# A planned one-core transformer block: other engine costs in the planner, and x tiles 4 and 5 transposed by DMA

## The chip, the cores and the metric

The kernel runs on one core of one Trainium2 chip. A core has five engines with a queue each: PE (TensorE, matmuls), ACT (ScalarE), DVE (VectorE), POOL (GpSimd) and SP (SyncE, which here only issues DMAs). An engine takes its instructions strictly in the order in which they were written into its queue; a wait at the head of a queue holds up all that stands behind it. The metric is the device time of one execution in microseconds.

## The reference

One block over 2048 tokens of width 1024, in bf16: multi-query attention with 32 heads of width 32 and one shared K and V, then a gated feed-forward part of width 3584.

```
h  = x + softmax(q k^T * 32**-0.5) v @ wo        # q, k, v from layernorm(x); k and v have one head
h2 = h + (sigmoid(g) * u) @ w_down               # g, u from layernorm(h) @ w_gate, w_up
```

## The kernel before

**Tiles.** There are 16 token tiles of 128. The first layer norm (`stats`, L325, with `ph` 0) takes tiles of x, and each normalised tile is transposed, either by PE over a PSUM bank (`mk_xT`) or by a DMA transpose (`x_by_dma`, L378, which first scales the tile on DVE). `TUNE["xd"]` says from which tile on the DMA does it: 6 before. From the transposed tiles come K and V (`mk_KV`) and Q (`mk_Qc` for the first two tiles, `mk_Q` for the others, which go out to `q_scratch` and are read back).

**Attention.** One "visit" is one key tile for half of the heads of one token tile. PE computes four score matmuls of 512 columns, which run side by side on four groups of 32 rows of the array (`emit_S`), into two of three pairs of PSUM banks; ACT does two exps of 1024 columns (L662), which write P to one of 12 slots of `Pr` (a few other buffers serve as slots at first); DVE adds the slot to `acc` (L637). There are 2 x 16 visits a token tile and 512 in all. Every eight key tiles, P·V (`mk_PV`) runs four matmuls side by side on four groups of 32 columns, and its result is taken into `oun` (L753, L757). At the end of each half the sums go through PE (`mk_SUM`), a reciprocal on DVE (L699), a write to `r_scratch` and four broadcast reads into `rb` (L702), and `OT` is the product (L716). The first two halves take their sums from matmuls with ones instead.

**The rest of a token tile.** The out-projection `mk_OP` adds to x in `h_sb` (L819). The second layer norm is `stats` with `ph` 1: bn_stats and bn_aggr, two casts (`mvb` L340, `mvr` L342) on DVE; eps, square root and reciprocal on POOL (`zb` L344, `dsb` L347, `rstd` L350); `hn` on DVE (L825); a DMA transpose to `hnT` (L840). The gate and up matmuls (`mk_GU`, here "gate/up") take seven groups of weights a tile from a ring of slabs in SBUF, which are loaded anew for nearly each tile (L902); ACT does tanh (L955) and DVE the product `hact` (L961). The down matmuls (`mk_D`, "down") are four groups of 28 a tile, added to `h_sb` (L998), and go out by L1005.

**Who sets the order.** None of this order is written by hand. `Plan` runs once while the program is built: it keeps for each engine the time from which it is free, gives every operation an occupancy and a latency in ns, and puts it into its engine's list. The four other engines always take the ready operation that can start first, by priority. PE's list is made by the loop at the end: a visit goes in as soon as the exp that frees its banks is known to have ended and ACT has less than `run` (900 ns) of work ahead; in between, PE is filled from the queues of groups (`PRIOS`, `held`), matmul by matmul, and each change of mode between plain, row-tiled and column-tiled matmuls adds `SWITCH`. Two PSUM banks, `F_ps`, serve all groups but the scores. So a wrong cost in the planner leaves no error in the result, only an order that meets waits the planner did not see. Numbers that matter here:

- the occupancy and latency of the three POOL steps, L343 to L352;
- `SWITCH` (L150), and `LATE` (L45), which adds ns to the landing of some DMAs by their key: `rb`, `hT`, `xt` (the keys of the slabs begin with `sl`, that of `r_scratch` is `rd`, but keys are compared without trailing digits);
- `h0`, `h1`: while a long group is about to end, DVE work of low priority (the adds) is held if it would overlap the stretch from `h0` to `h1` ns after that end;
- `qf`: which order of queues PE is filled from; `few`, `sum_few`, `pv_few`: at how many free P slots P·V and sums may interrupt or start outside the row mode; `swait`: how long PE may stay in column mode for a visit; `d_a`, `d_b`: when the down groups are due; `dall`: whether a down group waits for all of its weights; `eb`, `eq`: a bias in ns on the choice between ACT and DVE for emptying PSUM in the head.

Of the kernel before, what the change touches and what calls it, by code (L numbers as in the profile page):

```python
# [15 lines left out]
SEM = 75.0  # L16


TUNE = dict(swait=200, parts=2, raw=2, rl=0, nd=4, pc=16, rate=270, pace=280, xd=6, qf=0, dall=1, wo_late=1,
            nkn=3, few=2, rmin=700, hmin=1, h0=100, h1=100, hf=1.0, run=900, sum_few=2, pv_few=3, d_off=2,  # L20
            d_a=0, d_b=1, eb=450, eq=1000)


class Op:
# [16 lines left out]
class Plan:  # L41


    ENG = ("act", "dve", "pool", "sp")
    LATE = {"rb": 300.0, "hT": 400.0, "xt": 400.0}  # L45

    def __init__(self):
        self.lists = {e: [] for e in ("pe",) + self.ENG}
# [44 lines left out]
    def step(self, limit):  # L93
# [21 lines left out]
        if o.nbytes:  # L115
            if o.pace:
                self.pace_free = s + o.nbytes / TUNE["pace"]
            go = max(s + 1500.0, self.dma_free)
            self.dma_free = go + o.nbytes / TUNE["rate"]
            o.end = self.dma_free + 750.0 + self.LATE.get(o.key.rstrip("0123456789"), 0.0)  # L120
        else:
# [25 lines left out]
    return dict(occ=n / rate + fix - 90.0, lat=n / rate + fix + SEM)  # L147


SWITCH = 97.0  # L150


def bass_sequential_preLN__grouped_kv_mqa__glu_gated_glu__prompt_kernel(
# [16 lines left out]
    NT = S // P  # L170
# [13 lines left out]
    with ExitStack() as es:  # L184
# [3 lines left out]
        def SB(name, shape, dt=BF16):  # L188
            return EC(nc.sbuf_tensor(name, [P] + shape, dt))
# [13 lines left out]
        rb = SB("rb", [512], F32)  # L203
# [52 lines left out]
        def evac(fn_act, fn_dve, n, deps, prio, dve_rate=0.96, bias=0.0):  # L256
            now = pl.free["pe"]
            a = max(pl.free["act"], now) + sum(o.occ for o in pl.heap["act"]) + n / 1.2 + bias
            d = max(pl.free["dve"], now) + sum(o.occ for o in pl.heap["dve"] if o.prio <= prio) + n / dve_rate
            if a < d:  # L260
                return pl.op("act", fn_act, deps, prio=min(prio, 2), **t_act(n))
            return pl.op("dve", fn_dve, deps, prio=prio, **t_dve(n, dve_rate))

        def both(out_ap, in_ap):
            return (lambda: ACT.activation(out=out_ap, in_=in_ap, func=ACTF.Copy),
                    lambda: DVE.tensor_copy(out=out_ap, in_=in_ap))  # L266
# [57 lines left out]

        def stats(ph, tiles, srcs, deps, prio):  # L325
            t0, k = tiles[0], len(tiles)
            ag = []
            for t, src, dp in zip(tiles, srcs, deps):
                s = n_st[0] % 8
                n_st[0] += 1  # L330
                a = pl.op("dve", lambda s=s, src=src: DVE.bn_stats(st[:, s, 0, :], src[:, 0:512]), dp, prio=prio,  # L331
                          occ=600, lat=756, order=[st_user.get(s)])
                b = pl.op("dve", lambda s=s, src=src: DVE.bn_stats(st[:, s, 1, :], src[:, 512:1024]), dp, prio=prio,  # L333
                          occ=600, lat=756, order=[st_user.get(s)])
                c = pl.op("dve", lambda s=s, t=t: DVE.bn_aggr(mv[:, ph, t, :], st[:, s, :, :]), [a, b], prio=prio - 1,
                          occ=110, lat=284)
                st_user[s] = c
                ag.append(c)
            tk = slice(t0, t0 + k)
            d = pl.op("dve", lambda: DVE.tensor_copy(out=mvb[:, ph, tk, :], in_=mv[:, ph, tk, :]), ag, prio=prio - 1,  # L340
                      occ=90, lat=250)
            e = pl.op("dve", lambda: DVE.tensor_copy(out=mvr[:, ph, tk, :], in_=mvb[:, ph, tk, :]), [d], prio=prio - 1,  # L342
                      occ=90, lat=250)  # L343
            f = pl.op("pool", lambda: POOL.tensor_scalar(  # L344
                out=zb[:, ph, tk], in0=mvb[:, ph, tk, 1], scalar1=LN_EPS_BF16, scalar2=None, op0=ALU.add),
                [d], prio=prio - 1, occ=330, lat=440)
            g = pl.op("pool", lambda: POOL.tensor_tensor(  # L347
                out=dsb[:, ph, tk], in0=zb[:, ph, tk], in1=half[:, 0:k], op=ALU.pow), [f, c0], prio=prio - 1,
                occ=460 + 180 * k, lat=560 + 180 * k)
            h = pl.op("pool", lambda: POOL.tensor_tensor(  # L350
                out=rstd[:, ph, tk], in0=dsb[:, ph, tk], in1=negone[:, 0:k], op=ALU.pow), [g, c1], prio=prio - 1,
                occ=400 + 180 * k, lat=500 + 180 * k)  # L352
            return e, h

        sv1 = {}
        for tiles in ([0], [1], [2, 3], [4, 5], [6, 7], [8, 9], [10, 11], [12, 13], [14, 15]):
            r = stats(0, tiles, [x_sb(t) for t in tiles], [[x_ld[t]] for t in tiles], 3)
            for t in tiles:
                sv1[t] = r
        xnorm = {}  # L360
        xcent = {}
        for t in range(NT):
            if t >= TUNE["pc"]:
                xcent[t] = pl.op("pool", lambda t=t: POOL.tensor_scalar(
# [7 lines left out]
        def make_norm1(t, deps):  # L372
            dst, src, sc = xn[:, t % 2, :], x_sb(t), rstd[:, 0, t:t + 1]
            xnorm[t] = evac(lambda: ACT.activation(out=dst, in_=src, func=ACTF.Copy, scale=sc),
                            lambda: DVE.tensor_scalar(out=dst, in0=src, scalar1=sc, scalar2=None, op0=ALU.mult),
                            1024, [xcent[t], sv1[t][1]] + deps, 1, 3.2, bias=TUNE["eb"])

# [34 lines left out]
        def pe_op(fn, n, mode, deps, last_of_round=True):  # L412
            if mode != pl.pe_mode:
                pl.free["pe"] += SWITCH
                pl.pe_mode = mode
# [10 lines left out]
        def mk_xT(t):  # L426
# [6 lines left out]
            def after(b, last):  # L433
                src = F_ps[:, b, :].bitcast(BF16).rearrange("p (a b) -> p a b", a=DT)
                fa, fd = both(xnT[:, t // 4, :, (t % 4) * P:(t % 4 + 1) * P], src)
                xT_ev[t] = evac(fa, fd, 1024, [last], 2, 1.92, bias=TUNE["eb"])
                if t + 2 < NT:
                    if t + 2 < TUNE["xd"]:
                        make_norm1(t + 2, [last])
# [372 lines left out]
        def mk_OP(t, dc):  # L812
            def atoms(b):
                return [(mm(F_ps[:, b, :], OT[:, g, :], wo_sb[:, g, dc * 512:(dc + 1) * 512], g == 0, g == NG - 1),
                         512, "dense", []) for g in range(NG)]

            def after(b, last):
                sl = slice(dc * 512, (dc + 1) * 512)
                h_ev[(t, dc)] = pl.op("dve", lambda: DVE.tensor_tensor(  # L819
                    out=h_sb[:, t % NHB, sl], in0=F_ps[:, b, :], in1=h_sb[:, t % NHB, sl], op=ALU.add),  # L820
                    [last, xr_ld[t]], prio=1, **t_dve(512))
                if dc == 1:
                    op_last[t] = last
                    sv = stats(1, [t], [h_sb[:, t % NHB, :]], [[h_ev[(t, 0)], h_ev[(t, 1)]]], 3)
                    hnorm[t] = pl.op("dve", lambda: DVE.tensor_scalar(  # L825
                        out=hn[:, :], in0=h_sb[:, t % NHB, :], scalar1=mvr[:, 1, t, 0:1], scalar2=rstd[:, 1, t:t + 1],
                        op0=ALU.subtract, op1=ALU.mult), list(sv) + [hT_last.get(t - 1)],
                        prio=2, occ=400, lat=600)
                    load_hT(t)
                return [h_ev[(t, dc)]]  # L830

            def gate():
                return t in xr_ld and xr_ld[t].end is not None and (t == 0 or (t - 1) in hT_last)
            return Group("OP", atoms, lambda: [ot_ev[2 * t], ot_ev[2 * t + 1], wo_lds[0]], after, gate)
# [203 lines left out]
        while True:  # L1038
# [15 lines left out]
            if v < NV:  # L1054
                run = max(pl.free["act"], t) + sum(o.occ for o in pl.heap["act"])
# [97 lines left out]
        for e in lists:  # L1153
            n = 0
# [89 lines left out]
```

## Time and profile before

| | us |
|---|---|
| median of 3 runs (1126.56 to 1129.8) | 1127.76 |
| the profiled execution, as a run | 1125.96 |
| its span, first to last instruction | 1123.8 |
| PE busy / ACT busy / DVE busy / POOL busy | 1089.5 / 1013.0 / 827.8 / 69.4 |

| line | engine, what | count | mean ns | busy us |
|---|---|---|---|---|
| L662 | ACT exp | 1008 of 1024 | 1053 | 950.2 |
| L955 | ACT tanh | 112 | 619 | 69.4 |
| L637 | DVE add of P to `acc` | 450 | 1221, 1165 | 547.9 |
| L410 | PE gate/up, 128 columns | 7168 | 220 | 456.6 |
| L410 | PE down, 256 columns | 1792 | 273 | 233.7 |
| L410 | PE scores, 512 columns | 2048 | 387 | 203.2 |

A row has the busy time of a group, in which overlapping instructions count once. The mean of a matmul is its whole way through the pipeline, and the next one starts long before it has ended; so what a matmul costs is read from the distance between the starts of neighbours in the timeline, not from these means. PE, ACT and DVE work side by side from about 17 us on, when the first score group starts; the last exp ends at 1040.5 us, and after that PE works nearly alone.

### The profile page before, as it was taken

The page shows a single profiled execution, that of the slowest core. Times are in us where ns is not written, and L with a number is a line of the kernel's source. Part 1 is how long each engine was busy: PE and PEld are TensorE (multiplying, and loading weights), DVE is VectorE, ACT ScalarE, POOL GpSimd, SP SyncE. Part 2 cuts the span into 40 slices and gives each one's busy share as a digit, 9 for nine tenths or more (in the row PEclk, how much of TensorE's full clock was granted, in tenths as well). Part 3 has the DMA queues.
Part 4 walks back from the last instruction along what each step waited for, and adds up shares of the span by engine and source line. Part 5 has one row for each costly group of instructions (what it writes and reads, how often), then busy time and mean ns, then how long its engine had stood idle before and what let it go on. Part 6 is the DMA issues. An engine that isn't in the chain of part 4 may idle for free.

```text
span 1123.8 us, 34582 instructions
## 1 busy us (share of the span) xinstructions
PE 1089.5 (97%) x15032; PEld 737.6 (66%) x15032; DVE 827.8 (74%) x1040; ACT 1013.0 (90%) x1151; POOL 69.4 (6%) x97
## 2 busy tenths in 40 slices
PE   5899998999999999999999999999999999999999
PEld 4533554657676676757676676757666675767898
DVE  8728889587887869697886869698786868688311
ACT  4899999999999999999999999999999999999110
POOL 4200100010000101010000101010010101010000
PEclk9999998999999999999999999999999999999999
DMA  7882696666757485665757485665747476665993
GB/s 230 168 285 75 188 292 198 211 194 190 225 149 233 130 254 153 207 199 175 233 146 234 129 250 166 194 207 172 225 140 241 117 226 179 205 205 154 285 295 100
DMA packets 242230, 220.75 MB, mean 196 GB/s; under 512 B 45344, under 2 KB 228640, under 8 KB 242080
## 3 DMA queue, kind: packets, MB, share of 16 engines
q1 hardware_dynamic: 242080, 218.54, 65.1%
q8 instruction: 119, 1.95, 0.7%
q14 instruction: 31, 0.25, 0.1%
HBM read 203.55 MB, written 8.11 MB: 188 GB/s over the span
## 4 chain that ended last, share of the span: by engine, by line
PE 36%; ACT 28%; DVE 18%; issue 8%; POOL 4%; DMA 4%; SPq 1%; DVEq 0%
PE F_ps L410 31%; ACT Pr L662 26%; DVE acc L637 9%; PE S_ps L410 5%; ACT tnh L955 2%; DMA rb<-r_scratch 2%; POOL dsb L347 2%; DVE st L331 2%; POOL zb L344 2%; DVE st L333 2%; DVE hact L961 1%; DVE h_sb L819 1%; SPq L702 1%; POOL rstd L350 1%; DVE h_sb L998 1%
## 5 line engine op out<-in xcount | busy, mean ns | idle before, releaser
L662 ACT ACTIVATE Pr<-S_ps 128x1024 bf16<-128x1024 f32 x1008 | 950.2, 1053 | 19.9 <-PE S_ps L410 17.6
L637 DVE TENSOR_TENSOR acc<-acc,Pr 128x2048 bf16<-128x2048 bf16 x420 | 512.9, 1221 | 66.8 <-ACT Pr L662 51.1
L410 PE MATMUL F_ps<-hnT,ring 128*128 128x128 bf16 x6720 | 430.3, 220 | 7.6 <-issue 7.0
L410 PEld LDWEIGHTS F_ps<-hnT,ring 128*128 128x128 bf16 x6720 | 382.5, 98 | 67.0 <-issue 61.1
L410 PE MATMUL F_ps<-zone,hact 128*128 128x256 bf16 x1792 | 233.7, 273 | 0.0
L410 PE MATMUL S_ps<-QTb,kT 32*128 32x512 bf16 x2048 | 203.2, 387 | 5.2 <-ACT Pr L662 4.8
L410 PEld LDWEIGHTS F_ps<-zone,hact 128*128 128x128 bf16 x1792 | 160.0, 98 | 57.8 <-issue 42.0
L410 PE MATMUL F_ps<-Pr,Vt 128*32 128x512 bf16 x2016 | 127.1, 381 | 0.0
L410 PEld LDWEIGHTS S_ps<-QTb,kT 32*128 32x128 bf16 x2048 | 51.6, 91 | 114.7 <-ACT Pr L662 53.6
L955 ACT ACTIVATE tnh<-F_ps 128x512 f32<-128x512 f32 x112 | 69.4, 619 | 61.1 <-PE F_ps L410 61.1
L961 DVE SCALAR_TENSOR_TENSOR hact<-tnh,F_ps 128x512 bf16<-128x512 f32 x112 | 76.4, 683 | 54.5 <-PE F_ps L410 54.4
L410 PE MATMUL F_ps<-zone 128*128 128x512 bf16 (+3 forms) x584 | 76.7, 276 | 4.9 <-DVE Vt L266 2.1
L344 POOL TENSOR_SCALAR zb<-mvb 128x1 bf16<-128x1 bf16 (+1 forms) x25 | 20.2, 807 | 989.7 <-DVE mvb L340 989.5
L410 PEld LDWEIGHTS F_ps<-Pr,Vt 128*32 128x32 bf16 x2016 | 44.8, 96 | 55.3 <-issue 17.6
L410 PE MATMUL F_ps<-wo_sb,OT 128*128 128x512 bf16 x256 | 63.3, 380 | 0.7 <-DVE h_sb L998 0.4
L998 DVE SCALAR_TENSOR_TENSOR h_sb<-F_ps,h_sb 128x256 bf16<-128x256 f32 x64 | 26.9, 421 | 47.2 <-PE F_ps L410 47.2
L410 PEld LDWEIGHTS F_ps<-zone 128*128 128x128 bf16 x584 | 39.1, 98 | 33.0 <-issue 9.7
L757 DVE TENSOR_TENSOR oun<-F_ps,oun 128x512 f32<-128x512 f32 x32 | 22.0, 688 | 36.4 <-PE F_ps L410 36.4
L410 PEld LDWEIGHTS F_ps<-wo_sb,OT 128*128 128x128 bf16 x256 | 21.5, 97 | 28.0 <-issue 7.4
L637 DVE TENSOR_TENSOR acc<-Pr 128x2048 bf16<-128x2048 bf16 x30 | 35.0, 1165 | 0.0
L699 DVE RECIPROCAL r_sb<-F_ps 128x64 f32<-128x64 f32 x30 | 16.7, 558 | 21.4 <-PE F_ps L410 21.4
L347 POOL TENSOR_TENSOR dsb<-zb,cst 128x1 bf16<-128x1 bf16 (+1 forms) x25 | 29.8, 1195 | 1.9
(72 smaller groups left out, 324.5 us busy)
## 6 DMA issues: line engine op xcount, KB each, us to landing
ring<-in_B_w_gate_dram SPq DMA_DIRECT2D x308, 256.0 KB, 4.0
ring<-in_B_w_up_dram SPq DMA_DIRECT2D x304, 256.0 KB, 3.8
rb<-r_scratch SPq DMA_DIRECT2D x120, 64.0 KB, 2.8
zone<-in_B_w_down_dram SPq DMA_DIRECT2D x14, 512.0 KB, 4.6
Pr<-in_B_w_up_dram SPq DMA_DIRECT2D x24, 256.0 KB, 4.8
Pr<-in_B_w_gate_dram SPq DMA_DIRECT2D x20, 256.0 KB, 4.3
ring<-in_A_x_dram SPq DMA_DIRECT2D x16, 256.0 KB, 6.1
h_sb<-in_A_x_dram SPq DMA_DIRECT2D x16, 256.0 KB, 2.9
```

What stands on the lines that cost most here:

```text
L331: a = pl.op("dve", lambda s=s, src=src: DVE.bn_stats(st[:, s, 0, :], src[:, 0:512]), dp, prio=prio, occ=600, lat=756, order=[st_user.get(s)])
L333: b = pl.op("dve", lambda s=s, src=src: DVE.bn_stats(st[:, s, 1, :], src[:, 512:1024]), dp, prio=prio, occ=600, lat=756, order=[st_user.ge ...
L344: f = pl.op("pool", lambda: POOL.tensor_scalar(out=zb[:, ph, tk], in0=mvb[:, ph, tk, 1], scalar1=LN_EPS_BF16, scalar2=None, op0=ALU.add), ...
L347: g = pl.op("pool", lambda: POOL.tensor_tensor(out=dsb[:, ph, tk], in0=zb[:, ph, tk], in1=half[:, 0:k], op=ALU.pow), [f, c0], prio=prio - ...
L410: return lambda: PE.matmul(o, lhsT=l, rhs=r, start=start, stop=stop, **kw)
L637: add_op[(hf, kt)] = pl.op("dve", lambda: DVE.tensor_tensor(out=a, in0=in0, in1=slot, op=ALU.add), dp, prio=6, **t_dve(2048, 1.92))
L662: exps[u] = pl.op("act", lambda i=i, pb=pb: ACT.activation(out=slot[:, i * 1024:(i + 1) * 1024].rearrange("p (a b) -> p a b", a=2), in_=S_ ...
L699: rc = pl.op("dve", lambda: DVE.reciprocal(r_sb[:, :], F_ps[:, b, 0:64]), [last, rd_ld.get(hf - 1)], prio=0, occ=64 * 8 / 0.96 + 20, lat=6 ...
L757: oun_ev[(hf, part)] = pl.op("dve", lambda: DVE.tensor_tensor(out=o, in0=F_ps[:, b, :], in1=o, op=ALU.add), [last, oun_ev[(hf, part - 1)]] ...
L955: box["a"] = pl.op("act", lambda: ACT.activation(out=tnh[:, :], in_=F_ps[:, b, :], func=ACTF.Tanh, scale=0.5), [last, box.get("e")], prio= ...
L961: e = pl.op("dve", lambda: DVE.scalar_tensor_tensor(out=ho, in0=shape(tnh[:, :]), scalar=1.0, in1=shape(F_ps[:, b, :]), op0=ALU.add, op1=A ...
L998: e = pl.op("dve", lambda: DVE.scalar_tensor_tensor(out=h_sb[:, t % NHB, sl], in0=F_ps[:, b, 0:DW], scalar=0.5, in1=h_sb[:, t % NHB, sl], ...
```

## The change

Nothing is computed differently. The planner gets other costs and settings, and from them another order of all queues:

```diff
-TUNE = dict(swait=200, parts=2, raw=2, rl=0, nd=4, pc=16, rate=270, pace=280, xd=6, qf=0, dall=1, wo_late=1,
-            nkn=3, few=2, rmin=700, hmin=1, h0=100, h1=100, hf=1.0, run=900, sum_few=2, pv_few=3, d_off=2,
-            d_a=0, d_b=1, eb=450, eq=1000)
+TUNE = dict(swait=300, parts=2, raw=2, rl=0, nd=4, pc=16, rate=270, pace=280, xd=4, qf=2, dall=0, wo_late=1,
+            nkn=3, few=0, rmin=700, hmin=1, h0=100, h1=350, hf=1.0, run=900, sum_few=0, pv_few=4, d_off=2,
+            d_a=-1, d_b=0, eb=0, eq=700)
...
-    LATE = {"rb": 300.0, "hT": 400.0, "xt": 400.0}
+    LATE = {"sl": 400.0, "rd": 300.0, "rb": 300.0, "hT": 400.0, "xt": 400.0}
...
-SWITCH = 97.0
+SWITCH = 108.0
...
+            def slow(n, wait):
+
+                n += wait if ph and t0 < NT - 1 else 0
+                return dict(occ=n, lat=n + 100)
...
-                [d], prio=prio - 1, occ=330, lat=440)
+                [d], prio=prio - 1, **slow(330, 920))
...
-                occ=460 + 180 * k, lat=560 + 180 * k)
+                **slow(460 + 180 * k, 900))
...
-                occ=400 + 180 * k, lat=500 + 180 * k)
+                **slow(400 + 180 * k, 0))
```

`slow` makes the planner allow 920 ns more for `zb` and 900 ns more for `dsb` in the second layer norm, but for its last tile. With `xd` at 4, x tiles 4 and 5 go by DMA transpose too: 16 of PE's 48 transposes and two copies out of PSUM go, and two DMA transposes come. All other operations are the same ones in another order. Line numbers of the program after are six higher from there on.

## The prediction

> **What bounds the kernel now.** I read the page's busy shares first, then the busy time by stretches, then the start times in the timeline, and last the waits. PE (97%) and ACT (90%) are both near full, and the stretches show that this holds through the whole steady part:
>
> ```profile
> core 0: us, PE busy (x) PEld busy (x) DVE busy (x) ACT busy (x) POOL busy (x), PEclk, DMA share, GB/s
> 212.00:530.00 318.00, 314.91 (x4485) 214.91 (x4482) 248.51 (x286) 314.77 (x356) 16.59 (x15) 1.00 0.64 191
> 530.00:977.00 447.00, 441.33 (x6278) 301.31 (x6275) 347.51 (x399) 440.86 (x498) 23.64 (x21) 1.00 0.64 191
> 1038.00:1124.00 86.00, 82.98 (x1159) 75.35 (x1157) 21.81 (x38) 9.59 (x15) 1.34 (x3) 1.00 0.72 227
> ```
>
> The reader is to see PE and ACT at 99% in the middle, and PE alone at the end. Busy time overlaps, so I price by start-to-start distances of neighbours in the timeline (medians): a dense matmul of 128, 256, 512 columns takes 56, 109.5, 216 ns; a group of four score or P·V matmuls 216 ns; a sum group of four 29 ns; entering a tiled mode from dense adds 96 ns, leaving one 111 ns. An exp takes 904 or 921 ns back to back, half each, so 912; a tanh 478. With these, all PE work of the kernel comes to 1074.9 us. PE starts at 9.8 and the span ends 2.9 after its last start, so 1123.8 - 9.8 - 2.9 - 1074.9 = 36.2 us are stalls. Counting score groups ("visits", 512 of them, 32 a token tile), PE passes visit 32 at 85.7 us, 96 at 212.5 and the last at 1038.0. From 96 to the last that is 825.5 us: PE work 809.7, stalls 15.8. ACT has 830 x 0.912 + 90.5 x 0.478 = 800 us there. Per tile: elapsed 63.7, PE 62.4, ACT 61.7. **PE bounds the steady part, ACT stands 1% behind it.**
>
> Where the steady stalls come from, at one tile boundary:
>
> ```profile
> 245.52 1.23 DVE L637 TENSOR_TENSOR acc<-acc,Pr 128x2048 bf16<-128x2048 bf16 x1
> 247.88 0.55 DVE L825 TENSOR_SCALAR hn<-h_sb,mvr,rstd 128x1024 bf16<-128x1024 bf16 x1 [1.14 <-POOL rstd L350]
> 248.34 0.68 DVE L757 TENSOR_TENSOR oun<-F_ps,oun 128x512 f32<-128x512 f32 x1
> 249.13 0.89 PE L410 MATMUL F_ps<-hnT,ring 128*128 128x128 bf16 x13 [0.66 <-issue]
> 250.40 1.94 ACT L662 ACTIVATE Pr<-S_ps 128x1024 bf16<-128x1024 f32 x2 [0.70 <-PE S_ps L410]
> ```
>
> DVE stands 1.14 us at hn for GpSimd; behind it in DVE's queue is oun, which frees one of the two F_ps banks; PE gets the bank when oun has ended, and ACT then waits for PE. "issue" hides that. Such gaps before gate/up matmuls sum to 8.0 us over 13 tiles; 3.6 us more stand before the sum matmuls (behind h_sb, L998). The waits agree:
>
> ```profile
> DVE hn L825 <- POOL rstd L350: 16.0, 15, 1.2
> DVE OT L716 <- DMA rb<-r_scratch: 10.6, 13, 1.8
> ```
>
> One more hole is in the fill. PE runs four score groups with nothing between them, at ACT's pace, because no other work is ready:
>
> ```profile
> 187.04 0.61 PE L410 MATMUL S_ps<-QTb,kT 32*128 32x512 bf16 x4 [1.44 <-ACT Pr L662]
> 188.88 0.61 PE L410 MATMUL S_ps<-QTb,kT 32*128 32x512 bf16 x4 [1.22 <-ACT Pr L662]
> 191.88 0.80 PE L410 MATMUL F_ps<-hnT,ring 128*128 128x128 bf16 x6 [0.56 <-DMA hnT<-hn]
> ```
>
> From 183.4 to 191.9 this loses 6.4 us.
>
> **What the Trainium skill says.** "SBUF — State Buffer", section "Who interferes with whom": a VectorE instruction with two SBUF inputs and a GpSimd one that reads SBUF exclude each other for the whole instruction. The trace agrees: zb takes 220 ns in the first norm and 1035 beside the two-input adds of L637 (1221 ns each):
>
> ```profile
> L344 POOL TENSOR_SCALAR zb<-mvb 128x1 bf16<-128x1 bf16 x18 | 18.6, 1035 | 969.2 <-DVE mvb L340 969.0
> L344 POOL TENSOR_SCALAR zb<-mvb 128x2 bf16<-128x2 bf16 x7 | 1.5, 220 | 20.5 <-DVE mvb L340 20.5
> ```
>
> "Perfetto Trace Analysis", section "GPSIMD Engine Instruction", advises start-to-start spacings for GpSimd: from mvb's start to rstd's end they give 3.8 us in 12 of 16 tiles, against 2.0 to 2.7 in the first norm. The old plan allows 0.25 + 0.44 + 0.74 + 0.68 = 2.1, the new one 0.25 + 1.35 + 1.64 + 0.68 = 3.9, which is nearly what was measured. "TensorEngine Tiling", section "Key Properties", says that a change of tiling mode drains the array; the trace prices it at 96 and 111 ns, mean 103.5. The old plan has 97, the new 108.
>
> **The change, part by part.** No operation is removed or added except in the head; everything else is order. Counted in the two built programs:
>
> 1. GpSimd's latency and the rb chain (rd +300 ns). Between mvr and hn DVE now has mostly three instructions, two or three of them adds, where it had one add. Three adds fill 3.4 us, so hn should wait about 0.1 us. Worth up to 8.0 + 3.6 = 11.6 us of PE stalls; oun and h_sb no longer queue behind a waiting hn. The price is hn itself 1 us later, and who waits for that is the transpose on SP and then the next tile's gate/up: nothing, as 18 to 40 us of PE work stand between the out-projection and them in the new order, and in the trace of before hnT had landed 5.8 to 7.5 us early from the third tile on.
>
> 2. Mode changes: 1127 become 1157. 30 x 0.1035 = +3.1 us of PE, in the bound itself. 16 PE transposes fewer give back 16 x 0.056 = 0.9. Sum of PE work 1077.4 (+2.5).
>
> 3. Less filling per tile. Between visits 96 and 511 a tile gets on average 429 gate/up matmuls (448 before), 106 down (112), and 72.4 mode changes (70): 24.0 + 11.6 + out-projection 3.5 + scores 6.9 + P·V 6.9 + sums 0.5 + 7.5 = 61.0 us. It had 62.4. ACT per tile: 64 x 0.912 + 6.7 x 0.478 = 61.6. **The bound of the steady part changes from PE to ACT**, and PE gets 0.6 us of slack a tile. What is not filled in goes behind the last exp: 960 gate/up and 355 down matmuls instead of 765 and 308, 98.8 us instead of 82.7. There PE is alone, so these 16.1 us are on the path in full.
>
> 4. Head: x tiles 4 and 5 by DMA. SP's transposes wait for DVE's norm, with q_scratch stores and the later transposes queued behind; issue to landing is 3.3 us. PE runs 88 dense matmuls (6.2 us) before the next score group, so the scores are later: PE work ahead of visit 32 is 70.4 instead of 67.8. DVE has two PSUM copies (0.67 us each) fewer. I take the head's stalls as before (85.7 - 9.8 - 67.8 = 8.1 us); bounds 4 (the copies no longer behind statistics) and 12 (a transpose late).
>
> 5. The hole at 187 us: in the new order no two score groups stand side by side, as down matmuls of the first tile lie between those of this stretch. Worth 6.4, but ACT bounds that stretch too, which the sum below takes in.
>
> 6. Slab landings +400 ns, held adds (h1), paces: order only; DVE (74% busy) and DMA (65%) hide them. In the tail two slabs more are fetched than before, about 2 MB, 7 us at the 285 to 295 GB/s of that stretch, beside 16 us more PE work: no new wait. Bounds 0 and +3.
>
> The sum, by stages. Visit 32: 9.8 + 70.4 + 8.1 = 88.3 (was 85.7). To visit 96 ACT bounds: 128 x 0.912 + 10 x 0.478 = 121.5, plus 1.5 for unmatched starts, 123.0 (was 126.8; PE work 116.9). To visit 511 ACT has 830 x 0.912 + 87 x 0.478 = 798.6, PE 791.3; I add 0.3 us a tile for jitter, since a score group may be at most one exp early: 802.6, or 61.9 us a tile (bounds 0 and 1.2, the old PE stall on the new PE work, less the slack). Tail 98.8 + 0.5 + 2.9 = 102.2. Together **1116.1 us**, 7.7 under the span of 1123.8. That profiled execution took 1125.96 as a run and the median of three is 1127.76, 4.0 over the span; so 1120.
>
> **Rivals.**
> - *Matched engines lose what the waits gave* (20%). If each tile still stalls PE for 1.2 us, now at ACT, the steady part is 13 x 62.2 = 807 and the run 1124.5. For it: PE and ACT are 1% apart, with one exp of play. Against: 11.6 of the 15.8 us have one named cause that goes.
> - *Better* (14%). Jitter nil and head stalls 4: 1116.1 - 4 - 3.9 = 1108 span, 1112.
> - *Slower: the tiles keep their old length* (10%). The 16.1 us in the tail are paid for certain; they pay back only if the score groups come sooner. If P slots or banks (DVE's adds and copies, whose waits are unlike before) hold them, the steady part stays 825.5 and the run is 1139 + 4 = 1143. It decides from 62.5 us a tile upwards. Against: DVE is idle 13 of every 50 us, and waits for ACT (51.1 us at the adds), not the reverse.
> - *The new numbers change no order*: excluded, all five queues differ.
>
> **How the numbers follow.** The forecast (56%) is 1120, its own range 1116 to 1124. About 0.3%, 3.4 us, can be told from no change, so faster means under 1124.4, slower over 1131.1. Faster: 0.53 of the forecast's 0.56, 0.14, and half of the first rival, 0.10, make 0.77; same 0.13; slower 0.10. The range 1112 to 1128 leaves out the slower rival and some 7% of the rest.
>
> **What would show it.** hn's wait for rstd below 3 us in total (16.0 before); no gap before gate/up matmuls behind oun; visit 96 near 211 and the last score group near 1014; a PE-only end of about 102 us; ACT's idle time in the middle under 1 us a tile, and PE's stalls there put down to ACT. The forecast is wrong if the tiles take over 62.5 us, or if the tail shows DMA waits.

## The result, and the profile after

The changed kernel takes **1121.24 us** (median of four runs, 1120.97 to 1122.52), against 1127.16 for the kernel before in the same runs: ratio 0.9947, 95% interval 0.9926 to 0.9968. The forecast was 1120, faster. Its profiled span is 1118.9 us, 4.9 under the 1123.8 of before.

The stretches of the changed kernel, cut at its own visits 96 and last (columns as in the view of before):

```profile
core 0: us, PE busy (x) PEld busy (x) DVE busy (x) ACT busy (x) POOL busy (x), PEclk, DMA share, GB/s
210.00:530.00 320.00, 315.79 (x4514) 213.07 (x4517) 253.02 (x290) 319.51 (x366) 11.31 (x15) 1.00 0.64 194
530.00:955.00 425.00, 421.17 (x5919) 284.91 (x5924) 334.21 (x384) 424.23 (x484) 18.66 (x21) 1.00 0.64 189
1016.00:1119.00 103.00, 99.22 (x1400) 90.92 (x1399) 31.73 (x49) 11.61 (x18) 1.34 (x3) 1.00 0.71 216
```

In the first stretch ACT now has no gap to speak of (busy 319.5 of 320.0 us), while PE is idle for 4.2 of them; before, both had gaps (PE busy 314.9 and ACT 314.8 of 318.0). Recorded exps overlap, with a mean of 1053 ns before and 1193 after at start-to-start distances of 904 or 921, so ACT's busy time hides short waits. The stretch with PE alone holds 1400 matmuls instead of 1159 and is 17 us longer. The chain that ended last says the same in shares of the span, before and then after:

```profile
PE 36%; ACT 28%; DVE 18%; issue 8%; POOL 4%; DMA 4%; SPq 1%; DVEq 0%
```

```profile
ACT 63%; PE 25%; DVE 5%; issue 5%; DMA 2%; SPq 1%; DVEq 0%
```

POOL is gone from it, and ACT carries most of it. One tile boundary, first on DVE, then on POOL:

```profile
248.45 0.21 DVE L341 BATCH_NORM_AGGREGATE mv<-st 128x2 f32<-128x12 f32 x1
248.69 0.17 DVE L346 CAST mvb<-mv 128x2 bf16<-128x2 f32 x1
248.90 0.17 DVE L348 CAST mvr<-mvb 128x2 f32<-128x2 bf16 x1
...
252.83 0.45 DVE L831 TENSOR_SCALAR hn<-h_sb,mvr,rstd 128x1024 bf16<-128x1024 bf16 x1
```

```profile
248.95 0.22 POOL L350 TENSOR_SCALAR zb<-mvb 128x1 bf16<-128x1 bf16 x1 [63.67 <-DVE mvb L346]
249.26 0.56 POOL L353 TENSOR_TENSOR dsb<-zb,cst 128x1 bf16<-128x1 bf16 x1
249.89 0.55 POOL L356 TENSOR_TENSOR rstd<-dsb,cst 128x1 f32<-128x1 bf16 x1
```

Here the casts stand directly behind each other, and no add runs on DVE while GpSimd works, so `rstd` is there at 250.4, and `hn` comes at 252.8 without a wait for it. Only 4 of the 16 boundaries are like this one. At the other 12, adds run beside GpSimd, and the steps take 2.6 to 3.7 us from the start of `mvb` to the end of `rstd`; there `hn` stands behind the adds, as at 426 us:

```profile
426.26 1.24 DVE L643 TENSOR_TENSOR acc<-acc,Pr 128x2048 bf16<-128x2048 bf16 x1
...
427.75 2.54 DVE L643 TENSOR_TENSOR acc<-acc,Pr 128x2048 bf16<-128x2048 bf16 x2
430.21 0.54 DVE L831 TENSOR_SCALAR hn<-h_sb,mvr,rstd 128x1024 bf16<-128x1024 bf16 x1
```

```profile
428.00 1.37 POOL L356 TENSOR_TENSOR rstd<-dsb,cst 128x1 f32<-128x1 bf16 x1
```

In the whole kernel the 16.0 us that `hn` waited for `rstd` are 0.0. The old hole in the fill, too, has work in it; PE runs down matmuls (`zone,hact`) between the score groups:

```profile
185.07 0.40 PE L416 MATMUL S_ps<-QTb,kT 32*128 32x512 bf16 x4
...
187.27 0.28 PE L416 MATMUL F_ps<-zone,hact 128*128 128x256 bf16 x1
...
188.67 0.39 PE L416 MATMUL S_ps<-QTb,kT 32*128 32x512 bf16 x4 [1.11 <-ACT Pr L668]
188.99 1.48 PE L416 MATMUL F_ps<-zone,hact 128*128 128x256 bf16 x12
```

**The clock differs there too**, which the prediction did not look at. In the trace of before, the granted clock of PE was 0.50 from 186.9 to 197.1 us; in the trace of the change it was 1.00 throughout. From 191.9 to 197.1 us PE has no gap in either kernel, but 45 matmuls fall into it before and 77 after (the mixes differ), and a score group takes 0.61 us before and 0.39 or 0.40 after:

```profile
191.90:197.10 5.20, 5.20 (x45) 3.95 (x45) 4.02 (x4) 3.94 (x5) 0.00 (x0) 0.50 0.29 95
```

```profile
191.90:197.10 5.20, 5.20 (x77) 3.26 (x79) 4.54 (x6) 5.20 (x8) 0.00 (x0) 1.00 0.21 54
```

By estimate the kernel before loses some 2.6 us there, half of the 5.2, and the accounting below books them as stalls.

**Yet the stalls of the steady part have hardly fallen.** The waits (who, for whom: total us, count, longest us) show what took the place of DVE's wait. Before:

```profile
PEld S_ps L410 <- ACT Pr L662: 53.6, 130, 1.7
ACT Pr L662 <- PE S_ps L410: 17.6, 26, 2.6
```

After:

```profile
PEld S_ps L416 <- ACT Pr L668: 86.7, 249, 1.3
ACT Pr L668 <- PE S_ps L416: 5.9, 7, 2.8
```

ACT hardly waits for PE any more; PE's weight loads (PEld) wait for ACT about twice as often. These sums are no stalls, since PE can still be busy with earlier matmuls while a load waits.

The prediction's accounting makes this exact: span = PE's first start (9.8) + PE work of the built order + stalls + 2.9. Here it is for the two kernels and eight of the experiments, each from one traced execution (us; stalls are what the sum leaves over, so a lower clock counts among them; "tile" is the mean time from visit 96 to the last, "PE" and "ACT" their summed work in such a tile, by the prices of the prediction; e6's ACT is 61.57 less an estimated 3.4):

| kernel | visit 96 | last visit | span | end after it | tile | PE | ACT | PE work | stalls to visit 96 | steady stalls | `hn` waits |
|---|---|---|---|---|---|---|---|---|---|---|---|
| before | 212.5 | 1038.0 | 1123.8 | 85.8 | 63.66 | 62.43 | 61.70 | 1074.9 | 20.1 | 15.9 | 16.0 |
| after | 210.3 | 1016.1 | 1118.9 | 102.7 | 62.14 | 61.00 | 61.57 | 1077.4 | 13.1 | 14.6 | 0.0 |
| e1 | 211.3 | 1026.3 | 1111.7 | 85.5 | 62.84 | 62.43 | 61.70 | 1074.9 | 19.0 | 5.3 | 0.0 |
| e9 | 211.7 | 1025.3 | 1110.8 | 85.5 | 62.73 | 62.43 | 61.70 | 1074.9 | 19.3 | 3.9 | 0.7 |
| e5 | 212.1 | 1030.1 | 1117.1 | 87.0 | 63.07 | 62.43 | 61.70 | 1074.9 | 19.8 | 8.3 | 0.5 |
| e2 | 211.5 | 1024.5 | 1126.7 | 102.1 | 62.69 | 61.96 | 61.61 | 1077.5 | 25.7 | 9.4 | 2.0 |
| e3 | 211.8 | 1017.0 | 1127.4 | 110.4 | 62.09 | 60.69 | 61.57 | 1077.4 | 18.6 | 18.1 | 5.0 |
| e4 | 212.3 | 1024.6 | 1120.1 | 95.5 | 62.64 | 61.71 | 61.69 | 1077.4 | 17.5 | 11.9 | 0.0 |
| e10 | 211.1 | 1025.4 | 1120.6 | 95.2 | 62.79 | 61.73 | 61.70 | 1076.8 | 17.1 | 13.6 | 4.0 |
| e6 | 213.9 | 1016.2 | 1118.5 | 102.3 | 61.86 | 61.00 | 58.2 | 1077.4 | 16.8 | 11.1 | 0.0 |

The change's -4.9 us is +2.5 of PE work, -7.0 of stalls before visit 96, -1.3 of steady stalls and +0.8 at the end. The waits were priced at up to 11.6 us. The forecast itself let the steady stalls fall by less, from 15.9 to 11.3 us (802.6 less 791.3), since ACT would bound. They fell to 14.6. The experiments ask where the rest went.

### The profile page after: what moved, and what is told of

It reads as the page before. It is cut to its first block, busy times and chain, and to the rows that moved or that the text cites. A ratio compares the mean times of both kernels' runs of the same rounds, so it can differ in the third digit from the quotient of the medians.

```text
span 1118.9 us, 34515 instructions
## 1 busy us (share of the span) xinstructions
PE 1087.6 (97%) x14987; PEld 737.2 (66%) x15016; DVE 825.4 (74%) x1034; ACT 1005.9 (90%) x1155; POOL 57.8 (5%) x97
## 4 chain that ended last, share of the span: by engine, by line
ACT 63%; PE 25%; DVE 5%; issue 5%; DMA 2%; SPq 1%; DVEq 0%
ACT Pr L668 59%; PE F_ps L416 22%; ACT tnh L961 4%; PE S_ps L416 3%; DMA rb<-r_scratch 1%; DVE acc L643 1%; DVE st L339 1%; DVE st L337 1%; SPq L708 0%; DVE ring L374 0%; DVE ring L386 0%; DMA ring<-in_B_w_gate_dram 0%; DMA ring<-in_A_x_dram 0%; PE F_ps L435 0%; DVE oun L759 0%
## 5 line engine op out<-in xcount | busy, mean ns | idle before, releaser
L668 ACT ACTIVATE Pr<-S_ps 128x1024 bf16<-128x1024 f32 x1008 | 957.7, 1193 | 6.3 <-PE S_ps L416 5.9
L643 DVE TENSOR_TENSOR acc<-acc,Pr 128x2048 bf16<-128x2048 bf16 x420 | 513.3, 1222 | 53.6 <-ACT Pr L668 39.6
L416 PE MATMUL F_ps<-zone,hact 128*128 128x256 bf16 x1792 | 227.4, 273 | 0.1
L416 PEld LDWEIGHTS F_ps<-zone,hact 128*128 128x128 bf16 x1792 | 162.8, 98 | 47.3 <-issue 27.8
L961 ACT ACTIVATE tnh<-F_ps 128x512 f32<-128x512 f32 x112 | 85.9, 767 | 75.2 <-PE F_ps L416 75.2
L416 PE MATMUL F_ps<-Pr,Vt 128*32 128x512 bf16 x2016 | 133.4, 382 | 1.8 <-DVE h_sb L1004 1.0
L416 PEld LDWEIGHTS S_ps<-QTb,kT 32*128 32x128 bf16 x2048 | 51.5, 91 | 123.3 <-ACT Pr L668 86.7
L416 PE MATMUL F_ps<-zone 128*128 128x512 bf16 (+3 forms) x572 | 73.7, 273 | 3.4 <-DVE mv L341 1.0
L416 PE MATMUL F_ps<-wo_sb,OT 128*128 128x512 bf16 x239 | 60.4, 380 | 3.8 <-DVE oun L759 1.4
L350 POOL TENSOR_SCALAR zb<-mvb 128x1 bf16<-128x1 bf16 (+1 forms) x25 | 5.8, 233 | 986.8 <-DVE mvb L346 986.6
L266 DVE CAST hact<-F_ps 128x512 bf16<-128x512 f32 (+1 forms) x25 | 16.3, 653 | 17.1 <-PE F_ps L416 15.2
```

The costliest lines, as they stand in the source:

```text
L350: f = pl.op("pool", lambda: POOL.tensor_scalar(out=zb[:, ph, tk], in0=mvb[:, ph, tk, 1], scalar1=LN_EPS_BF16, scalar2=None, op0=ALU.add), ...
L416: return lambda: PE.matmul(o, lhsT=l, rhs=r, start=start, stop=stop, **kw)
L643: add_op[(hf, kt)] = pl.op("dve", lambda: DVE.tensor_tensor(out=a, in0=in0, in1=slot, op=ALU.add), dp, prio=6, **t_dve(2048, 1.92))
L668: exps[u] = pl.op("act", lambda i=i, pb=pb: ACT.activation(out=slot[:, i * 1024:(i + 1) * 1024].rearrange("p (a b) -> p a b", a=2), in_=S_ ...
L961: box["a"] = pl.op("act", lambda: ACT.activation(out=tnh[:, :], in_=F_ps[:, b, :], func=ACTF.Tanh, scale=0.5), [last, box.get("e")], prio= ...
```

## The experiments

The ratios are to the kernel before, with their 95% intervals. It took 1125.72 us beside e1 to e4, 1126.44 beside e5 to e8 and 1124.19 beside e9 to e12, so across these three groups the ratios are to be compared and not the times.

**e1: take the wait away, and nothing else.** `hn` scales by the variance instead of 1/sqrt, so it doesn't need GpSimd, and its wait for `rstd` is left out of the program; the plan stays that of before, and GpSimd still does its steps. What this kernel leaves out is the right scale of the second layer norm. The lines that matter:

```diff
-  scalar1=mvr[:, 1, t, 0:1], scalar2=rstd[:, 1, t:t + 1],
+  scalar1=mvr[:, 1, t, 0:1], scalar2=mvr[:, 1, t, 1:2],
...
-  prio=2, occ=400, lat=600)
+  prio=2, occ=400, lat=600); hnorm[t].skip = sv[1]
...
-  if d.eng == e and e == "pe":
+  if d.eng == e and e == "pe" or d is o.skip:
```

> The kernel before with its order untouched in every queue; only hn of the second layer norm takes its scale from mvr (the variance) instead of rstd, so that DVE does not stand there for GpSimd (the second norm's scale is therefore the variance; the three GpSimd steps still run). Theory (the gain of the change is the wait for GpSimd, which ran through DVE to PE): the 11.6 us of PE stalls behind oun and h_sb go, the tiles shrink from 63.7 to about 62.8 us (PE work 62.4), and the run takes 1115 to 1119 us. Rival (the stalls are only re-labelled, since ACT is 1% behind PE): under 4 us gain, 1123 to 1127.

Measured: 1113.65 us, 0.9899 (0.9884 to 0.9914). The place in DVE's queue where before stood 1.14 us, in e1:

```profile
245.51 0.54 DVE L825 TENSOR_SCALAR hn<-h_sb,mvr 128x1024 bf16<-128x1024 bf16 x1
245.97 0.68 DVE L757 TENSOR_TENSOR oun<-F_ps,oun 128x512 f32<-128x512 f32 x1
```

Steady stalls fall from 15.9 to 5.3 us. So the wait and its way over `oun` and the F_ps bank to PE are shown, and so is its price, 10.6 us against 11.6 worked out. One wait in DVE's queue, 16.0 us in sum, off the engine that bounds, was worth 1% of the kernel; and this cut alone gains more than the whole change.

**e9: end the wait without leaving anything out.** In the plan of before, after planning, the two casts are put directly behind `bn_aggr` in DVE's list, so GpSimd starts before the next add does.

```diff
+  if ph:
+      moved.append((c, d, e))      # bn_aggr, mvb, mvr
...
+  for c, d, e in moved:
+      for o in (e, d):
+          pl.lists["dve"].remove(o)
+          pl.lists["dve"].insert(pl.lists["dve"].index(c) + 1, o)
```

> The kernel before, planned with its old costs and with PE's, ACT's and SP's queues untouched; in DVE's finished list the casts mvb and mvr of the second norm stand directly behind bn_aggr instead of behind one and two adds. GpSimd's chain then starts 1 us earlier and zb meets no add (0.3 instead of 1.36 us), so rstd should be there when hn comes. Theory (the wait at hn is worth some 12 us, and the changed kernel gives half of it back at its end): tiles near 62.8 us, run 1112 to 1116, clearly below the changed kernel. Rival (as in e5, hn in another place costs new waits): 1117 to 1121.

Measured: 1114.11 us, 0.9908 (0.9895 to 0.9921). `hn` waits 0.7 us in all. The boundary on DVE and on POOL:

```profile
241.58 0.17 DVE L340 CAST mvb<-mv 128x2 bf16<-128x2 f32 x1
241.78 0.17 DVE L342 CAST mvr<-mvb 128x2 f32<-128x2 bf16 x1
241.86 3.90 DVE L639 TENSOR_TENSOR acc<-acc,Pr 128x2048 bf16<-128x2048 bf16 x3
245.67 0.54 DVE L827 TENSOR_SCALAR hn<-h_sb,mvr,rstd 128x1024 bf16<-128x1024 bf16 x1
```

```profile
241.84 0.22 POOL L344 TENSOR_SCALAR zb<-mvb 128x1 bf16<-128x1 bf16 x1 [56.97 <-DVE mvb L340]
242.14 1.37 POOL L347 TENSOR_TENSOR dsb<-zb,cst 128x1 bf16<-128x1 bf16 x1
243.59 1.25 POOL L350 TENSOR_TENSOR rstd<-dsb,cst 128x1 f32<-128x1 bf16 x1
```

GpSimd's last two steps are slow beside the adds, but the chain now lies wholly under three of them. **This version leaves nothing out and is faster than both kernels**: its interval lies just under that of the change (0.9926 to 0.9968), though the two were not timed side by side. Against it the changed kernel reaches its last visit 9.2 us earlier and pays 17.2 us more after it.

**e5: the same wait ended the other way.** `hn` is put two places later in DVE's list.

```diff
+  for o in hnorm.values():
+      i = pl.lists["dve"].index(o)
+      pl.lists["dve"].insert(i + 2, pl.lists["dve"].pop(i))
```

> The kernel before, planned with all its old costs; only hn of the second norm stands two instructions later in DVE's finished list, behind the copy or add that frees an F_ps bank. No wait is taken away. Theory (DVE's queue is what carries GpSimd's wait to PE, and the rest of the change costs what this gains over it): as without the wait, tiles near 62.8 us, 85.5 us at the end, run 1113 to 1117, faster than the changed kernel. Rival (hn that comes later holds up the transpose and the next tile's gate/up): 1120 or more.

Measured: 1117.73 us, 0.9926 (0.9909 to 0.9943), just above the expected range. It gains less than e9, and the waits suggest why: DVE's queue now stands for a DMA instead. `OT` waits for `rb` 20.7 us in all, against 10.6 before and 2.9 in e9. At one boundary this reaches PE; that it makes up the whole difference is not shown:

```profile
863.12 0.69 DVE L716 TENSOR_TENSOR OT<-oun,rb 128x512 bf16<-128x512 f32 x1 [1.50 <-DMA rb<-r_scratch]
...
864.87 0.42 DVE L998 SCALAR_TENSOR_TENSOR h_sb<-F_ps,h_sb 128x256 bf16<-128x256 f32 x1
865.57 0.81 PE L410 MATMUL F_ps<-wo_sb,OT 128*128 128x512 bf16 x3 [1.06 <-DVE h_sb L998]
```

**e2: only the GpSimd costs in the planner** (`slow` for `zb` and `dsb`), all else of before.

```diff
-  [d], prio=prio - 1, occ=330, lat=440)
+  [d], prio=prio - 1, **slow(330, 920))
...
-  occ=460 + 180 * k, lat=560 + 180 * k)
+  **slow(460 + 180 * k, 900))
```

> The kernel before with the planner's new GpSimd costs alone. By the built order: PE work 1077.5, 62.0 us a tile beside ACT's 61.6, 97.9 us of PE work after the last exp, and five score groups that stand beside one another. Theory: hn's wait is gone, tiles of 62.4, visit 96 near 210, run 1120 to 1125. Rival (the new SWITCH is what made the gain): no gain, 1126 to 1129.

Measured: 1128.36 us, 1.0022 (1.001 to 1.0033): **slightly slower**, against the expectation. The wait does go (2.0 us left), and steady stalls fall to 9.4. But the planner fills less into the tiles; the work that is left over runs at the end:

```profile
212.00:1024.00 812.00, 805.54 (x11425) 549.36 (x11442) 643.16 (x737) 808.94 (x918) 38.85 (x39) 1.00 0.65 192
1024.00:1127.00 103.00, 98.56 (x1411) 90.73 (x1409) 24.57 (x42) 12.16 (x19) 1.34 (x3) 1.00 0.72 224
```

PE work grows by 2.6 us with some two dozen mode changes more, stalls at the end by 1.2, and up to visit 96 stalls are 5.6 us longer: less is filled in there too, but visit 96 comes only 1.0 us sooner. The three, 9.4 us, more than eat the gain of 6.5.

**e3: only the price of a mode change** in the planner.

```diff
-SWITCH = 97.0
+SWITCH = 108.0
```

> The kernel before with SWITCH 108 alone. By the built order: 60.7 us of PE work a tile against ACT's 61.6, 106.8 us of PE work after the last exp. Theory: hn's wait of about 1 us a tile stays and now stops ACT too, so tiles stay above 62.4, and the run is slower than before: 1129 to 1136. Rival (SWITCH made the gain): 1119 to 1123.

Measured: 1129.37 us, 1.0038 (1.0023 to 1.0053), slower as expected, but not by the expected way: the tile is 62.09 us and not above 62.4, and `hn`'s waits fall from 16.0 to 5.0 us, though nothing in this edit aims at them. Its stretches and waits:

```profile
212.00:1017.00 805.00, 792.22 (x10825) 527.56 (x10843) 637.01 (x729) 804.11 (x918) 32.50 (x39) 1.00 0.61 182
1017.00:1127.00 110.00, 106.90 (x1441) 97.55 (x1441) 28.89 (x48) 11.31 (x18) 1.34 (x3) 1.00 0.63 193
```

```profile
DVE hn L831 <- POOL rstd L356: 5.0, 7, 1.5
PEld S_ps L416 <- ACT Pr L668: 83.6, 238, 1.0
```

ACT is full (804.1 of 805 us) while PE has 12.8 us without work; those wait at the end. PE's work in a tile is 60.69 us here, 0.9 under ACT's, and the tile stays at 62.09. Filling less than the tile has room for gives away PE time here: the end takes 110.4 us instead of 85.8.

**e4: the change with the old price of a mode change.**

```diff
-SWITCH = 108.0
+SWITCH = 97.0
```

> The changed kernel with SWITCH back at 97. By the built order PE 61.7 and ACT 61.7 us a tile, 92.0 us after the last exp (98.8 in the changed kernel). Theory (the tile takes about 0.5 us more than the larger of the two): tiles of 62.3, steady part 808, run 1114 to 1118, faster than the changed kernel. Rival (the longer drain in the planner is part of the gain, since matched engines need slack on PE): 1122 to 1126.

Measured: 1121.70 us, 0.9967 (0.9953 to 0.9981), between the two expected ranges, nearer to the rival's. PE's work in a tile and ACT's are equal (61.71, 61.69), and the tile takes 62.64, not 62.3; the end is 7.2 us shorter than the change's, and the last visit 8.5 us later. Against the change's 0.9947 the intervals overlap: what the price of a mode change (`SWITCH`) adds to the other settings cannot be told from nothing by these runs.

**e10: only the TUNE line of the change** (`xd`, `qf`, `dall`, `few` and so on as in the change's diff), with the old costs.

> The changed kernel's settings (TUNE, xd 4 among them) with all old costs: no GpSimd wait known to the planner, SWITCH 97, old landings. By the built order PE 61.7 us a tile, 92.0 us after the last exp. Theory (the settings shape the head and the end, the costs take the wait away): hn waits in most tiles again, tiles near 62.8, run 1120 to 1126. Rival (the settings alone are the gain): 1117 to 1119.

Measured: 1122.69 us, 0.9988 (0.9981 to 0.9995), in the expected range. Only 4.0 us of `hn`'s wait remain, and not a wait in most tiles as I had expected: in this order most of it goes although the planner knows nothing of it. Steady stalls are 13.6 all the same: with PE and ACT equal (61.73, 61.70) the tile takes 62.79.

**e11 and e12: e9's reordering on top of e3 and of e10**, to see if the wait is what these still lose. The edit is that of e9.

> e3 (SWITCH 108 alone in the kernel before) with the casts directly behind bn_aggr as in e9. PE has 60.7 us a tile against ACT's 61.6, 106.8 us after the last exp. Theory (the wait at hn costs time only as long as PE's queue is full; here ACT has caught up): at most 3 us below e3, 1126 to 1130, and slower than the kernel before. Rival (the wait is worth the same everywhere): 1117 to 1121.

> e10 with the casts directly behind bn_aggr: the changed kernel's settings, the old costs, and no wait at hn. Theory: its end is 9.3 us longer than that of e9 and its tiles at most 0.5 us shorter, 6 us in 13, so it comes out 2 to 5 us above e9, 1115 to 1119. Rival (the settings close the hole at 187 us and win): 1109 to 1112.

Measured: e11 1128.58 us, 1.004 (1.0027 to 1.0053); e12 1121.57 us, 0.9977 (0.9969 to 0.9985). Neither contrast is clean, since the wait only fell from 5.0 to 2.3 us and from 4.0 to 3.0; e12 missed its expectation. What they do show: in e11 the wait halves, and steady stalls don't fall (18.1, then 19.7).

**e6 and e7: is ACT the bound?** From the second token tile on, the exps take 480 columns of each bank instead of 512; 32 columns of each are left out. In e6 in the changed kernel, in e7 in that of before.

```diff
-  out=slot[...].rearrange("p (a b) -> p a b", a=2), in_=S_ps[:, pb:pb + 2, :],
+  out=slot[...].rearrange("p (a b) -> p a b", a=2)[:, :, 0:480 if hf >= 2 else 512],
+  in_=S_ps[:, pb:pb + 2, 0:480 if hf >= 2 else 512],
```

> The changed kernel with every exp from the second token tile on covering 960 of its 1024 columns (the other columns of P keep older values), order untouched: 53 ns less per exp by ACT's rate, so 58.2 us of ACT work a tile instead of 61.6, beside 61.0 of PE work. Theory (ACT bounds the changed kernel's tiles): tiles go from 62.1 to 61.3 to 61.6 us and the run to 1109 to 1114. Rival (PE and its waits bound it): less than 3 us gained.

> The same shortened exps (960 of 1024 columns from the second token tile on) in the kernel before. Theory (PE bounds the tiles of before, 62.4 us of work and DVE's wait): at most 3 us gained, 1123 to 1127. Rival (ACT is in the bound there too): 1114 to 1120, as much as in the changed kernel.

Measured: e7 0.9986 (0.9977 to 0.9995), e6 0.9919 (0.99 to 0.9938). Before, ACT's work is nearly worthless, as PE's bound demands (e7's tile is 63.66 us, as before). In the changed kernel it is worth about 3 us (0.9947 less 0.9919, of 1127). As these two intervals overlap, that is hardly clear of the noise, and whether it is more than before is open; it is in any case far from the some 3.4 us *a tile* taken off ACT. The traced execution of e6 took 1120.70 us, 4.0 above the median of 1116.72. Its stretch:

```profile
214.00:1016.00 802.00, 795.02 (x11292) 539.00 (x11301) 633.56 (x728) 785.36 (x918) 31.18 (x39) 1.00 0.65 193
```

```profile
PEld S_ps L416 <- ACT Pr L668: 38.7, 92, 1.1
```

ACT has air now, PE's waits for it fall from 86.7 to 38.7 us, and yet the tile only falls from 62.14 to 61.86, 0.86 above PE's work. Perhaps the order, planned for exps of the old length, holds it there; that was not tested. Where those 0.86 us arise I did not find out.

**e8: x tiles 4 and 5 by DMA alone.**

```diff
-  xd=6
+  xd=4
```

> The kernel before with xd 4 alone: x tiles 4 and 5 by DMA transpose. By the built order PE work 1074.3 us (0.6 less), 72.3 instead of 67.8 us of it ahead of visit 32, tiles and end as before. Theory (the head is no part of the gain): 1125 to 1129, or within 2 us of the kernel before. Rival (the two copies fewer on DVE free the head): 1120 to 1124.

Measured: 1131.04 us, 1.0043 (1.0027 to 1.006), slower, which neither theory expected. In the traced execution (1133.58 us, 2.5 above the median) visit 32 comes at 93.7 us instead of 85.7, with PE's work ahead of it at 72.3. PE in the head:

```profile
24.24 6.61 PE L416 MATMUL F_ps<-zone 128*128 128x128 bf16 x79
30.91 0.40 PE L416 MATMUL S_ps<-QTb,kT 32*128 32x512 bf16 x4
...
43.90 1.01 PE L416 MATMUL F_ps<-zone 128*128 128x256 bf16 x4 [2.24 <-DMA zone<-ring]
```

79 dense matmuls stand ahead of a score group, and later a load is late; from 43.3 to 50.1 us the granted clock was 0.50 as well. In the changed kernel visit 32 comes at 86.7 in spite of the same `xd` (86.3 in e4, 86.7 in e10), so other settings of its TUNE line (the order of queues, `eb`, `eq`) mend the head; which of them was not separated. But e6, whose head has the same order as that of the changed kernel, reached visit 32 only at 90.9, so a microsecond or two between two single traces says little here.

## Why the prediction was right, and where its steps were off

**In short:** the time and the sign were right. In the steady part the cause (`hn`'s wait) and its going were right, but what this yields was overrated by 3.2 us, and the part went nearly the way of the first rival: 805.8 us, where that rival had 807 and the forecast 802.6. That the time came out at the forecast all the same is partly luck, since other terms were off the other way. Stage by stage against a span of 1116.1: visit 32 1.6 us earlier than I put it (86.7 for 88.3), from there to visit 96 0.6 longer, the steady part 3.2 longer, the end 0.5 longer; the run stands 2.3 over the span instead of 4.0. Together that is about +1 us, the 1121.24 for 1120.

1. *hn's wait, up to 11.6 us.* Right: it is 0.0 in the changed kernel, and in the order of before its removal alone gives 10.6 (e1). Right too is the way: at most boundaries adds now stand between `mvr` and `hn`. But the planner's higher cost for GpSimd, which I credited, is by itself slower than before (e2), and without it most of the wait goes as well (e10, e3). The times that it allows occur only in part: before, `zb` mostly ran into the adds (mean 1035 ns); now it starts beside a short cast and takes 229. `dsb` and `rstd` still run into adds at 12 of the 16 boundaries, and their means stay near twice what they take without an add (0.56 and 0.55 us). The rule behind this is in the Trainium skill, "SBUF — State Buffer", section "Who interferes with whom" (named in the prediction), and both numbers of `zb` agree with it.

```profile
L350 POOL TENSOR_SCALAR zb<-mvb 128x1 bf16<-128x1 bf16 x18 | 4.1, 229 | 967.1 <-DVE mvb L346 967.0
L353 POOL TENSOR_TENSOR dsb<-zb,cst 128x1 bf16<-128x1 bf16 x18 | 19.4, 1081 | 1.3
L356 POOL TENSOR_TENSOR rstd<-dsb,cst 128x1 f32<-128x1 bf16 x18 | 17.4, 969 | 1.3
```

2. *Mode changes.* PE work +2.5 us is a count of the built order at the prediction's prices and enters the accounting as such. It is not measured: the parts add up in every kernel, because stalls are the rest. No run tests it alone.

3. *Less filling; the bound goes from PE to ACT; 61.9 us a tile.* **This is the term that was mis-sized.** I had 61.57 us of ACT's work and 0.3 for jitter; the tile is 62.14, so the jitter is 0.57, close to the first rival's 62.2 (1.2 us of stalls a tile; 1.13 measured). Of the 1.13, 0.57 are PE's slack under ACT and 0.56 a loss beyond it. (The price of 912 ns for an exp is a little high: distances near 904 and near 921 are not half each, but 409 and 237 before, 525 and 194 after. With that, ACT's work is some 0.2 us a tile less, the slack 0.35 and the loss 0.8.) PE's stalls a tile go with what PE has to do beyond ACT: with 0.7 us more than ACT 0.30, 0.41 and 0.64 (e9, e1, e5), with 0.35 more 0.73 (e2), with as much 0.92, 1.05 and 0.88 (e4, e10, e12), with 0.57 less 1.13 (the change), with 0.9 less 1.40 and 1.52 (e3, e11). Part of this is plain: where PE has less to do than ACT, it must wait for the difference. These are different orders, and e3 and e10 to e12 still have 2.3 to 5.0 us of `hn`'s wait, so this is a regularity and not a proof; before (1.22, with the wait in it) doesn't belong to it. So **the gain of the missing wait was mostly given back in the steady part**, whose stalls only fall from 15.9 to 14.6 us. The forecast had foreseen part of that, with 7.3 us of slack under ACT and 3.9 of jitter; the jitter is what it had too small. In the waits, PE's weight loads now stand longer for ACT (53.6 us in sum before, 86.7 after). Why two nearly matched engines lose this much stays open. That ACT "becomes the bound" is at best half true: relieved in e6 it gives about 3 us, hardly clear of the noise.

4. *Head.* To take the stalls as before was too much in this trace; visit 32 came 1.6 us sooner than forecast. e8 shows that the risk named there (more dense work ahead of the scores, a late load) is real, and the changed kernel that other settings offset it, mostly: e6 reached visit 32 at 90.9.

5. *The hole at 187 us.* Filled, as forecast; with it and the head, stalls before visit 96 fall by 7.0 us, more than the change's whole net gain of 4.9. But the forecast priced the hole by its waits alone, and by the estimate above some 2.6 us of what went is PE at half the clock. This goes with the order of the kernel and not with chance: all four runs of the changed kernel had a mean clock of 1.00; beside e1 to e4 all runs of before had 0.994 to 0.997, and those of e3 0.998 to 1.00. Nor can I say which setting fills the hole: e4, with all but `SWITCH`, has 17.5 us of stalls before visit 96, and the change 13.1, but e4's clock was 0.50 from 177.5 to 184.3 us. What brings the clock down was not tested.

6. *Slabs, holds.* Taken at nothing, with +3 as the bound. The end (102.7 for 102.2) leaves no more than 0.5 us for it there. They were not tried alone, nor was the later `rd` of the first term.

The slower rival had 62.5 us a tile as the point of decision; e2 is a case of it, at 62.69 with an end of 102.1, and is slower. The changed kernel passed it by 0.36 us a tile, 4.7 us in 13 tiles.

## What to carry to other kernels

When one engine bounds and works through to the end, moving its work behind another engine's last instruction is worth nothing by itself: only its work and its stalls count, so account for every plan as work plus stalls before believing in shorter tiles. Expect a loss when two engines become equal: PE stalled 0.9 to 1.1 us a tile where its work was equal to ACT's, and 0.3 to 0.6 where it had 0.7 us of 62 more. That this margin is the cause is not shown, as the orders differ. And where a short chain on a side engine blocks an in-order queue, start the chain earlier by hand (e9, two casts moved, 0.9908) before giving a whole planner new costs, which move everything else too. Last, look at the granted clock of each stretch before putting a price on a hole in it.

## What the runs showed of the hardware

- GpSimd's steps of one column change with what runs beside them on DVE: `dsb` took 0.56 us and `rstd` 0.55 where DVE ran no add (changed kernel at 249 us), 1.37 and 1.25 beside the adds of e9, while `zb` took 0.22 in both; in e9 it started at 241.84, just ahead of the first add at 241.86. The Trainium skill, "SBUF — State Buffer", section "Who interferes with whom", says that the order of issue decides who blocks; `zb` in e9 agrees, and `dsb` and `rstd`, which started while the adds ran, show the other side.
- Exps of 1024 columns stand about 904 or 921 ns apart back to back, in both kernels; the share near 904 is 63% before and 73% after. In e6 and e7, with 960 columns, it is 851 or 868. No view gave a cause for the two distances.
- The granted clock fell to 0.50 for stretches of 3.4 to 10.2 us in the traces of before and of e1 to e10 and e12, and not at all in those of the changed kernel and of e11. In such a stretch a score group took 0.61 us instead of 0.39 or 0.40. No run here separates what causes it.
